# A planned attention and ReGLU kernel: blocks of 2 and 4 tiles, transposing transfers one tile earlier, and a planner with other due times

## The chip, the cores and the metric

The kernel runs on one core of one Trainium2 chip. The metric is the device time of one execution in microseconds (us), less is better. The kernel before takes 240.97 us, the median of three runs (240.74 to 241.13).

## The reference, cut to what matters

Chunked attention with memory rows on 4 batches of 8 heads, 768 positions of 64 values; then a gated feed-forward layer on the 3072 rows of 512 that come out.

```
for c in range(nc):                       # 24 chunks of 32 positions
    q_c = q[:, :, c_start:c_end]
    k_full = concat([mem_k, k[:, :, c_start-16 : c_end+8]])     # 8 + up to 56 keys
    v_full = concat([mem_v, v[:, :, c_start-16 : c_end+8]])
    a = softmax(q_c @ k_full.T / 8)
    out[:, :, c_start:c_end] = a @ v_full
x = out as 3072 rows of 512
return (relu(x @ w_gate) * (x @ w_val)) @ w_out    # 512 -> 1536 -> 512
```

## The kernel before

The 3072 rows are 24 tiles of 128, six to a batch of the reference. A tile `a` passes through these steps, and the names are those of the planner's list:

- `qk`: two loads on POOL's queue, k and q of the tile, cast to bf16 on the way (`load_qk`, L257). Batch 0 (tiles 0 to 5) has its own loads of pairs.
- `t`, `tc`: k and q turned so that the head's 64 values lie on partitions. Up to tile 10 TensorE does it (`qk_t`, L279, four transposes each for k and for q), and ACT or DVE copies the result out of PSUM. From tile `LATE_QK` = 11 on one transposing transfer on SP's queue does both (`qk_transfer`, L283), and only the copy of the keys into `kT` is left, `tc`, on ACT or DVE (L79, L81).
- `s`: scores, 32 small matmuls (L310). They need the copied keys of the tile and of the one behind it, because a chunk sees 8 keys to its right.
- `max`, `sub`, `exp`, `sum`, `rec`, `nrm`: softmax on DVE and ACT.
- `p`, `pc`: P turned. Up to tile 9 on TensorE with a copy (L359), from `LATE_P` = 10 on by a transposing transfer on SP (`p_transfer`, L363).
- `v`, `x`: values, 16 matmuls (L389; batch 0 has its own form), copied to `xT`.

Values stand in two large tiles `v_bd`, one for each parity of the batch. For a batch POOL issues two large loads and two small ones (`vl`, `ve`, L184), and eight copies of the memory's rows (`mr`, L167; batch 1's on SP). From the loads, 16 copies on ACT or DVE (`up`, `upper`) fill the rows that chunks share. The loads of batch 3 come only when tile 11's values are through; a small memset on DVE (`hold`, L684) that the planner puts behind tile 17's `tc` keeps them back further.

The feed-forward layer goes by blocks of 2 or 4 tiles. For a block, 24 products `f` (gate and value in turn, L408; four matmuls of 256 or 512 columns each) go through four PSUM slots (`fps`); a relu on ACT frees the gate's slot (L414), a multiplication on DVE the value's (L420). Then the products `o` with the second weights, in triples of matmuls (L433), four triples to a tile, through the same slots; ACT copies each tile out and stores it (`oc`, L79, L440). The slots go round in the order of use: a product takes the slot of the one four before it.

The order of everything is written by a planner in the kernel, when it is built. It goes through modelled time with a cost for each step, and gives each free engine the step of highest priority whose operands are due by its estimates. What comes out is one fixed order for each engine. On the chip each engine takes its instructions in this order and waits where an operand isn't there; the modelled times play no part any more. For a load the estimate is the end of a modelled queue plus a constant; for a transposing transfer the end of the same queue, and its users are due `LAND` or `LAND_P` us after that:

```
LAND = {a: 4.0 if a < 16 else 3.5 if a < 19 else 2.0 for a in range(NT)}
LAND_P = {a: 3.0 if a < 14 else 2.5 if a < 18 else 2.0 for a in range(NT)}
...
queue_end = max(queue_end, t + 1.5) + {"t": 2.6, "pc": 1.3}[key[0]]
done[key] = queue_end + 1.0
```

SP holds, after a few loads and the eight rows of batch 1, only transposing transfers. `pace` keeps the transposes on PE of later tiles from coming too early, by the place of their block; `pace_t` keeps a transfer behind the scores of five tiles before.

Of the kernel before, what the change touches and what calls it, by code (L numbers as in the profile page):

```python
# [19 lines left out]
def kernel(  # L20
# [27 lines left out]
    KW = CH + NMEM  # L48
    CTX = 16 + CH + 8
    NSET = 2  # L50
    BLOCKS = [2, 2, 2, 4, 4, 4, 4, 2]
    GROUPS = [(0, 2), (2, 6), (6, 9), (9, 12)]
    BAND0 = 48
    UT = 3

    LATE_QK, LATE_P = 11, 10

    KEY_RUNS = ((0, CH, 0), (KW, 64, CH), (CH, KW, CTX))
    assert sum(BLOCKS) == NT and NMEM == 8 and D == 64 and H == 8
# [455 lines left out]


    ISSUE, SLACK = 1.5, 1.0
    LAND = {a: 4.0 if a < 16 else 3.5 if a < 19 else 2.0 for a in range(NT)}
    LAND_P = {a: 3.0 if a < 14 else 2.5 if a < 18 else 2.0 for a in range(NT)}

    def pace_t(a):
        return [("s", a - 5)]
# [136 lines left out]
    load_v_nat(5)  # L659
    for par in range(2):  # L660
        load(("vm", par), 256, 0.3, lambda par=par: mem_values(par))
    for a, i in late[:5]:
        load_qk_op(a, i)
    for i in range(2):
        load(("wo", i), 768, 4.1, lambda i=i: load_out(i))
    for b in range(1, B):
        deps = ([("z0", hp, c0) for hp in range(HP) for c0 in range(0, NCH, 8)] if b > 1 else [("z1", hp) for hp in range(HP)]) + ([("v", TPB * (b - NSET + 1) - 1)] + ['hold'] if b > NSET else [])
        if b == 1:
            for n in range(2 * HP):
                op(("mr", b, n), {"SP": 0.72}, lambda e, b=b, n=n: mem_rows(nc.sync, b, n),  # L670
                   deps + [(("vm", 0), 0.2), (("vm", 1), 0.2)], (0,))
        for par in range(2):
            load_v_op(b, par, deps)
        if b == 2:
            for n in range(2 * HP):
                load(("mr", 2, n), 192, 0.22, lambda n=n: mem_rows(nc.gpsimd, 2, n),
                     deps + [(("vm", 0), 0.2), (("vm", 1), 0.2)])
        for a, i in late[(5, 20, 26)[b - 1]:(20, 26, 36)[b - 1]]:
            load_qk_op(a, i)
    for n in range(2 * HP):  # L680
        load(("mr", 3, n), 192, 0.22, lambda n=n: mem_rows(nc.gpsimd, 3, n),
             deps + [(("vm", 0), 0.2), (("vm", 1), 0.2)])

    op("hold", {"DVE": 0.1}, lambda e: nc.vector.memset(v_bd[1][0:2 * CH, 0, 0, :].bitcast(F32), 0.0), [("v", 2 * TPB - 1)],  # L684
       prio=(0,), after=[("tc",17,1)])
# [6 lines left out]
    def schedule():  # L692
        done, started, times = {}, set(), [0.7]
        free = {e: 0.7 for e in ("PE", "ACT", "DVE", "SP", "POOL")}
        queue_end, flying, gives = 0.0, [], [(WARM + 0.15, "fps")]
        room["fps"] -= 1
        heapq.heappush(times, WARM + 0.15)
        todo = {e: [] for e in free}
        order, n_load = [], 0
        names = lambda o: [d[0] if timed(d) else d for d in o["deps"]] + o["after"]  # L700
        missing = {k: len(set(names(o))) for k, o in ops.items()}
        users = {}
        for k, o in ops.items():
            for d in set(names(o)):
                users.setdefault(d, []).append(k)

        def offer(k):
            for e in ops[k]["eng"]:
                bisect.insort(todo[e], (ops[k]["prio"], k), key=lambda x: x[0])

        for k in ops:
            if not missing[k]:
                offer(k)

        def ready(o, t, margin=0.0):
            if any(d not in started for d in o["after"]):
                return False
            for d in o["deps"]:
                d, lag = d if timed(d) else (d, 0.0)
                if d not in done or done[d] + lag + margin > t + 1e-9:  # L720
                    return False
            return all(room[r] >= o["take"].count(r) for r in o["take"])

        while len(started) < len(ops) + len(loads):
            t = heapq.heappop(times)
            while times and times[0] <= t + 1e-9:
                heapq.heappop(times)
            for g in [g for g in gives if g[0] <= t + 1e-9]:
                gives.remove(g)
                room[g[1]] += 1  # L730
            flying = [f for f in flying if f > t]
            moved = True
            while moved:
                moved = False
                for e in ("POOL", "PE", "ACT", "DVE", "SP"):
                    if free[e] > t + 1e-9:
                        continue
                    if e == "POOL":
                        if n_load == len(loads):
                            continue  # L740
                        o = loads[n_load]
                        if len(flying) >= 8 or not ready(o, t):
                            continue
                        n_load += 1
                        key = o["key"]
                        if o["n"]:
                            end = t + 0.62 + 0.27e-3 * o["n"]
                            queue_end = max(queue_end, end + 0.8) + o["work"]
                            flying.append(queue_end + 1.0)
                            done[key] = queue_end + (1.2 if n_load < 8 else 4.5 if key[:2] == ("vl", 1) else 2.4 if n_load < 45 else 6.0 if key[0] == "vl" else 4.0)  # L750
                        else:
                            end = done[key] = t + max(o["work"], 0.6)
                        fn = o["fn"]
                    else:
                        o = None
                        soon = False
                        for _, key in todo[e]:
                            late_pe = e == "PE" and t > 36.0 and ops[key]["prio"][0] == 1
                            if ready(ops[key], t, MARGIN if late_pe else 0.0):
                                o = None if soon and key[0] in ("up", "z0") else ops[key]  # L760
                                break
                            soon = soon or ready(ops[key], t + 0.3)
                        if o is None:
                            if e == "PE" and 1.3 < t < WARM:
                                order.append((t, lambda: idle_product(256)))
                                free[e] = t + (0.213 if t < 9.0 else 0.11)
                                heapq.heappush(times, free[e])
                            elif e == "PE" and t <= 1.3:
                                heapq.heappush(times, 1.31)
                            continue  # L770
                        for x in o["eng"]:
                            todo[x].remove((o["prio"], key))
                        d = o["eng"][e]
                        d, lat = d if isinstance(d, tuple) else (d, d)
                        d *= (1.8 if e == "PE" and t < 8.0 and key[0] in ("t", "p", "sh", "f") else 1.0)
                        end = t + d
                        done[key] = end + 0.25 if e == "PE" else t + lat + 0.08

                        if e == "SP" and key[0] in ("t", "pc"):
                            queue_end = max(queue_end, t + 1.5) + {"t": 2.6, "pc": 1.3}[key[0]]  # L780
                            done[key] = queue_end + 1.0
                        elif queue_end > t and key[0] == "oc":
                            queue_end += 0.7
                        fn = lambda o=o, e=e: o["fn"](e)
                        for g in o["give"]:
                            g, lag = g if isinstance(g, tuple) else (g, 0.0)
                            gives.append((done[key] + lag, g))
                            heapq.heappush(times, done[key] + lag)
                    for r in o["take"]:
                        room[r] -= 1  # L790
                    started.add(key)
                    for k in users.get(key, ()):
                        missing[k] -= 1
                        if not missing[k]:
                            offer(k)
                    order.append((t, fn))
                    free[e] = end
                    lags = {d[1] for k in users.get(key, ()) for d in ops[k]["deps"] if timed(d) and d[0] == key}
                    for x in [end] + [done[key] + lag + m for lag in lags | {0.0, 0.2, 1.5} for m in (0.0, MARGIN)]:
                        heapq.heappush(times, x)  # L800
                    moved = True
            assert times, [k for k in ops if k not in started][:20]
        return order
# [33 lines left out]
```

## Time and profile before

| | |
|---|---|
| median of three runs | 240.97 us |
| the profiled execution | 240.65 us |
| its span on the core | 238.9 us |
| granted TensorE clock | 0.998 |
| PE, DVE, ACT, POOL busy | 232.5, 145.3, 135.5, 77.4 us |
| transposing transfers on SP | 13 of q and k, 14 of P |
| first product of tiles 6 to 9, 10 to 13, 14 to 17, 18 to 21 (us from the span's start) | 85.47, 120.61, 153.93, 188.99 |

PE is TensorE's matmuls, ACT ScalarE, DVE VectorE, POOL GpSimd and SP SyncE; L with a number is a line of the kernel before. The duration of a matmul includes its way through the array, so durations of neighbours overlap, and it is the distance from one start to the next that adds up to the span. An idle time in square brackets names what ended the wait before an instruction.

### The profile page before, as it was taken

Reading aid. Unit: us, or ns where it says so; the run is one execution under the profiler, and the core shown is the slowest. Engines: PE = TensorE matmul, PEld = TensorE weight load, DVE = VectorE, ACT = ScalarE, POOL = GpSimd, SP = SyncE. Lnnn points to the kernel's source line nnn. Section 1 sums busy time; section 2 is a strip of 40 time slices with the busy share of each in tenths; the row PEclk is TensorE's granted clock in tenths of the full one; section 3 lists DMA queues with packets and bytes.
Section 4 is the critical chain, followed back from the end, with each engine's and each line's share of the span. In section 5 each row is a group of like instructions: output and inputs, shape, how many; then the busy total and the mean of one; then the engine's idle time right before and its main releaser. Section 6 shows DMA issues by size and latency. Waiting matters only on the chain.

```text
span 238.9 us, 6437 instructions
## 1 busy us (share of the span) xinstructions
PE 232.5 (97%) x2654; PEld 137.7 (58%) x2654; DVE 145.3 (61%) x292; ACT 135.5 (57%) x284; POOL 77.4 (32%) x102
## 2 busy tenths in 40 slices
PE   7898999999999999999999999999999999999994
PEld 5577887785589644455544444444555444445873
DVE  6674876987888389994279851599960043410430
ACT  7577777866885456897566851365523233312422
POOL 8975779313920374700094552100000000000000
PEclk9999999999999999999999999999999999999999
DMA  6999999999999999996199999995121300012102
GB/s 74 171 179 202 201 166 161 206 133 125 190 166 138 131 156 118 122 129 136 70 141 101 135 154 91 113 209 64 27 43 47 127 4 0 0 47 88 44 3 88
DMA packets 103069, 26.88 MB, mean 113 GB/s; under 512 B 94080, under 2 KB 99968, under 8 KB 103040
## 3 DMA queue, kind: packets, MB, share of 16 engines
q0 software_dynamic: 76128, 14.65, 92.7%
q1 hardware_dynamic: 23312, 5.53, 23.2%
q10 hardware_dynamic: 3600, 6.29, 8.4%
q8 instruction: 21, 0.34, 0.7%
q14 instruction: 8, 0.07, 0.2%
HBM read 28.55 MB, written 6.29 MB: 146 GB/s over the span
## 4 chain that ended last, share of the span: by engine, by line
PE 93%; DMA 2%; POOL 2%; issue 1%; ACT 1%; ACTq 0%; POOLq 0%
PE v_ps L408 27%; PE g_ps L408 26%; PE out_ps L433 26%; PE xT_ps L389 3%; PE s_ps L310 2%; DMA v_n<-in_v_dram 2%; PE idle_ps L140 2%; PE vs_ps L216 2%; PE xT_ps L382 2%; PE qk_ps L279 1%; PE pT_ps L359 1%; POOL qk_p L229 1%; PE qk_ps L238 1%; PE xT_ps L375 1%; POOL v_n L200 0%
## 5 line engine op out<-in xcount | busy, mean ns | idle before, releaser
L420 DVE TENSOR_TENSOR gvT<-v_ps,g_relu 128x256 f16<-128x256 f32 (+1 forms) x96 | 53.0, 554 | 48.7 <-PE v_ps L408 35.1
L408 PE MATMUL v_ps<-xT,w_val_sb 128*128 128x256 f16 (+1 forms) x384 | 78.2, 326 | 0.1
L408 PE MATMUL g_ps<-xT,w_gate_sb 128*128 128x256 f16 (+1 forms) x384 | 78.1, 326 | 0.0
L414 ACT ACTIVATE g_relu<-g_ps 128x256 f16<-128x256 f32 (+1 forms) x96 | 47.0, 490 | 41.5 <-PE g_ps L408 39.8
L433 PE MATMUL out_ps<-w_out_sb,gvT 128*128 128x512 f16 (+2 forms) x300 | 65.8, 371 | 0.0
L408 PEld LDWEIGHTS <-w_gate_sb 128*128 128x128 f16 x384 | 36.9, 98 | 24.8
L408 PEld LDWEIGHTS <-w_val_sb 128*128 128x128 f16 x384 | 35.9, 98 | 22.5 <-issue 0.5
L433 PEld LDWEIGHTS <-gvT 128*128 128x128 f16 x300 | 27.6, 97 | 29.5
L79 ACT COPY o_sb<-out_ps 128x512 f32<-128x512 f32 (+2 forms) x25 | 14.2, 568 | 29.6 <-PE out_ps L433 19.4
L323 DVE TENSOR_REDUCE mx<-s_ps 128x8 f32<-128x512 f32 x24 | 16.4, 685 | 13.9 <-PE s_ps L310 13.5
L338 ACT ACTIVATE p_exp<-dif 128x256 f16<-128x256 f32 (+2 forms) x72 | 19.6, 339 | 6.3 <-DVE dif L330 6.1
L184 POOL DMA_DIRECT2D v_bd<-in_v_dram x12 | 11.0, 924 | 33.6 <-DVE v_bd L684 19.2
L342 DVE TENSOR_REDUCE sm<-p_exp 128x8 f32<-128x512 f16 x24 | 16.4, 683 | 5.0 <-ACT p_exp L338 4.8
L257 POOL DMA_DIRECT2D qk_b<-in_k_dram x18 | 16.2, 902 | 9.7 <-DMA v_bd<-in_v_dram 5.4
L257 POOL DMA_DIRECT2D qk_b<-in_q_dram x18 | 16.2, 899 | 9.7 <-DMA v_bd<-in_v_dram 7.2
L79 ACT COPY v_bd<-v_bd 24x768 f16<-24x768 f16 (+1 forms) x23 | 18.5, 823 | 1.2 <-ACT o_sb L79 0.9
L353 DVE TENSOR_TENSOR p_n<-p_exp,rinv 128x512 f16<-128x512 f16 x24 | 16.5, 686 | 0.3
L330 DVE TENSOR_TENSOR dif<-s_ps,mx 128x512 f32<-128x512 f32 x24 | 16.2, 674 | 0.2
L79 ACT CAST xT<-xT_ps 128x512 f16<-128x512 f32 x17 | 10.0, 586 | 8.5 <-PE xT_ps L389 7.3
L167 POOL DMA_DIRECT2D v_bd<-vmem x16 | 10.2, 645 | 12.4 <-DMA qk_b<-in_q_dram 6.1
L140 PE MATMUL idle_ps<-idle 128*128 128x256 bf16 x69 | 11.3, 314 | 1.1 <-DVE warm L477 1.1
L389 PEld LDWEIGHTS <-v_bd 128*128 128x128 f16 x288 | 9.8, 96 | 3.6
(60 smaller groups left out, 165.6 us busy)
## 6 DMA issues: line engine op xcount, KB each, us to landing
out_dram<-o_sb ACTq DMA_DIRECT2D x23, 256.0 KB
qk_b<-in_k_dram POOLq DMA_DIRECT2D x18, 128.0 KB, 8.0
qk_b<-in_q_dram POOLq DMA_DIRECT2D x18, 128.0 KB, 8.9
v_bd<-in_v_dram POOLq DMA_DIRECT2D x6, 384.0 KB, 11.2
w_out_sb<-in_moe_w_out_dram POOLq DMA_DIRECT2D x2, 768.0 KB, 10.5
qk_p<-in_k_dram POOLq DMA_DIRECT2D x3, 256.0 KB, 5.3
qk_p<-in_q_dram POOLq DMA_DIRECT2D x3, 256.0 KB, 6.3
v_n<-in_v_dram POOLq DMA_DIRECT2D x6, 128.0 KB, 6.5
```

What stands on the lines that cost most here:

```text
L79: nc.scalar.copy(o, i)
L257: nc.gpsimd.dma_start(qk_b[a][:, 1 - i], bass.AP(tensor=x.tensor, offset=x[b, 0, 128 * t, 0].offset, ap=[[D, 128], [S * D, H], [1, D]]))
L323: nc.vector.reduce_max(SM[a, "mx"], s4, axis=AX.X)
L330: nc.vector.tensor_tensor(out=SM[a, "dif"].rearrange("p (m r) a s -> p r m a s", r=2), in0=S_ps.pop(a).rearrange("p r (m a) s -> p r m a s ...
L338: nc.scalar.activation(p[:, :, :, s0:s0 + k1 - k0], dif[:, :, :, k0:k1], ACT.Exp, scale=SCALE)
L342: nc.vector.reduce_sum(SM[a, "sm"], SM[a, "p"], axis=AX.X)
L353: nc.vector.tensor_tensor(out=P_n[a], in0=SM.pop((a, "p")), in1=rinv_b, op=ALU.mult)
L389: nc.tensor.matmul(ps[:, hp, r], lhsT=v_bd[b % NSET][:, hp, 4 * t + g, :], rhs=x[:, hp, r], start=True, stop=True)
L408: nc.tensor.matmul(ps, lhsT=w[:, f, 128 * m:128 * m + 128], rhs=xTs[blk][:, f, :], start=(f == 0), stop=(f == NFC - 1))
L414: nc.scalar.activation(st["r", m], st.pop((0, m)), ACT.Relu)
L420: nc.vector.tensor_tensor(out=st["gv"][:, m, :], in0=st.pop((1, m)), in1=st.pop(("r", m)), op=ALU.mult)
L433: nc.tensor.matmul(st["o", t, c], lhsT=st["gv"][:, m, 128 * t:128 * t + 128], rhs=w_out_sb[:, m, c[0]:c[1]], start=(m == 0), stop=(m == ND ...
```

## The change

The list of blocks splits tiles 6 to 9 into 2 + 2. Transposing transfers do q and k from tile 10 and P from tile 9, so there are 14 and 15 of them. The order of loads becomes a list (`ORDER`: numbers are loads of k or q, `w` a half of the second weights, `v` the values of a batch, `m` its memory rows): batch 2's values now stand after 18 loads of k and q where they stood after 20, batch 3's after 26 in both. The planner's estimates change: a new rule with `turn` for when a transposing transfer ends, users due 4.5 us (`t`) and 3.5 us (`pc`) after it, and smaller constants behind loads. `pace` is as it was, but its lead of 44 us for blocks from the fifth on now holds for tiles 8 and 9.

```diff
-    BLOCKS = [2, 2, 2, 4, 4, 4, 4, 2]
+    BLOCKS = [2,2,2,2,2,4,4,4,2]
...
+    ORDER = [5, 'w0', 'w1', 'v1', 13, 'v2', 'm2', 8, 'v3', 10, 'm3']
...
-    LATE_QK, LATE_P = 11, 10
+    LATE_QK, LATE_P = 10, 9
...
-    LAND = {a: 4.0 if a < 16 else 3.5 if a < 19 else 2.0 for a in range(NT)}
-    LAND_P = {a: 3.0 if a < 14 else 2.5 if a < 18 else 2.0 for a in range(NT)}
+    LAND = {a: 4.5 for a in range(NT)}
+    LAND_P = {a: 3.5 for a in range(NT)}
...
+    def v_deps(b):
+        z = [("z0", hp, c0) for hp in range(HP) for c0 in range(0, NCH, 8)] if b > 1 else [("z1", hp) for hp in range(HP)]
+        return z + ([("v", TPB * (b - NSET + 1) - 1), "hold"] if b > NSET else [])
+    def mem_deps(b):
+        return v_deps(b) + [(("vm", 0), 0.2), (("vm", 1), 0.2)]
...
+    for step in ORDER:
+        if isinstance(step, int):
+            for a, i in late[n_qk:n_qk + step]:
+                load_qk_op(a, i)
+            n_qk += step
+            continue
...
-                            done[key] = queue_end + (1.2 if n_load < 8 else 4.5 if key[:2] == ("vl", 1) else 2.4 if n_load < 45 else 6.0 if key[0] == "vl" else 4.0)
+                            done[key] = queue_end + (1.2 if n_load < 8 else 4.5 if key[:2] == ("vl", 1) else 2.4 if n_load < 45 else 3.5 if key[0] == "vl" else 2.5)
...
-                            queue_end = max(queue_end, t + 1.5) + {"t": 2.6, "pc": 1.3}[key[0]]
-                            done[key] = queue_end + 1.0
+                            double = key[0] == "t"
+                            busy = queue_end > t + 1.2
+                            begin = max(t + 1.2 + (3.0 if busy else 0.2), turn)
+                            if queue_end > begin:
+                                turn = begin + (3.8 if double else 2.7)
+                                queue_end += 1.6 if double else 0.9
+                            else:
+                                turn = begin + (1.5 if double else 0.9)
+                            done[key] = turn + 0.3
```

The fixed order that the planner writes is the same as before on PE up to the second block's out products (60 us in the profile). Some places where it differs after that, with tiles in brackets:

| engine | before | after |
|---|---|---|
| ACT, first steps of tiles 14 to 17's block | exp(18), oc(13), relu 0, exp(19), relu 1, tc(22), relu 2, exp(20), relu 3, tc(23) | exp(18), tc(22), oc(13), relu 0, exp(19), relu 1, tc(23), exp(20), relu 2 |
| DVE | max(15), sub(15), hold | max(14), sub(14), hold |
| copies `up` of batch 3's second load, in the block of tiles 10 to 13 | from relu 7 on ACT and gate 6 on DVE on | from relu 4 and gate 4 on |
| SP | t(11 to 15), pc(10 to 13), t(16), pc(14), t(17, 18), pc(15 to 17), t(19 to 23), pc(18 to 23) | t(10 to 14), pc(9 to 12), t(15), pc(13), t(16 to 18), pc(14 to 17), t(19 to 23), pc(18 to 23) |
| PE, scores and values around 114 to 122 us | s(14) far ahead, v(14), s(15), s(16), block of 10 to 13 | v(13), s(14), s(15), s(16), block of 10 to 13, in it v(14) |

More of the change, by code (lines that the diff above doesn't have):

```diff
@@ L661 @@
         load(("vm", par), 256, 0.3, lambda par=par: mem_values(par))
[L662 to L668, printed above, removed]
-            for n in range(2 * HP):
[L670 to L682, printed above, removed]
+    def v_deps(b):
[3 more added lines that the diff above has]
+        return v_deps(b) + [(("vm", 0), 0.2), (("vm", 1), 0.2)]
+    n_qk = 0
+    for step in ORDER:
[4 more added lines that the diff above has]
+            continue
+        kind, b = step[0], int(step[1])
+        if kind == "w":
+            load(("wo", b), 768, 4.1, lambda b=b: load_out(b))
+        elif kind == "v":
+            for par in range(2):
+                load_v_op(b, par, v_deps(b))
+        else:
+            for n in range(2 * HP):
+                load(("mr", b, n), 192, 0.22, lambda b=b, n=n: mem_rows(nc.gpsimd, b, n), mem_deps(b))
+    if "m1" not in ORDER:
+        for n in range(2 * HP):
+            op(("mr", 1, n), {"SP": 0.72}, lambda e, n=n: mem_rows(nc.sync, 1, n), mem_deps(1), (0,))
     op("hold", {"DVE": 0.1}, lambda e: nc.vector.memset(v_bd[1][0:2 * CH, 0, 0, :].bitcast(F32), 0.0), [("v", 2 * TPB - 1)],
@@ L694, in schedule @@
         free = {e: 0.7 for e in ("PE", "ACT", "DVE", "SP", "POOL")}
-        queue_end, flying, gives = 0.0, [], [(WARM + 0.15, "fps")]
+        queue_end, turn, flying, gives = 0.0, 0.0, [], [(WARM + 0.15, "fps")]
         room["fps"] -= 1
@@ L779, in schedule @@
                         if e == "SP" and key[0] in ("t", "pc"):
-                            queue_end = max(queue_end, t + 1.5) + {"t": 2.6, "pc": 1.3}[key[0]]
-                            done[key] = queue_end + 1.0
+                            double = key[0] == "t"
[4 more added lines that the diff above has]
+                                queue_end += 1.6 if double else 0.9
+                            else:
+                                turn = begin + (1.5 if double else 0.9)
+                            done[key] = turn + 0.3
                         elif queue_end > t and key[0] == "oc":
```

## The prediction

> **What bounds the kernel now.** First the busy shares and the chain of work that ended last, from the page:
>
> ```profile
> PE 232.5 (97%) x2654; PEld 137.7 (58%) x2654; DVE 145.3 (61%) x292; ACT 135.5 (57%) x284; POOL 77.4 (32%) x102
> ...
> PE 93%; DMA 2%; POOL 2%; issue 1%; ACT 1%; ACTq 0%; POOLq 0%
> ```
>
> TensorE is the bound. Busy shares hide small gaps, so I then read the distance from start to start in the timeline of PE (start, duration, line, shapes, count):
>
> ```profile
> 46.55 0.60 PE L408 MATMUL g_ps<-xT,w_gate_sb 128*128 128x256 f16 x4
> ...
> 49.61 0.39 PE L375 MATMUL xT_ps<-pT,vmem 128*128 128x128 f16 x4
> ...
> 50.53 0.40 PE L359 MATMUL pT_ps<-band,p_n 128*128 128x128 f16 x4
> 50.77 0.60 PE L408 MATMUL v_ps<-xT,w_val_sb 128*128 128x256 f16 x4
> ...
> 56.05 0.61 PE L279 MATMUL qk_ps<-ident_b,qk_b 128*128 128x128 bf16 x8
> 56.50 3.40 PE L433 MATMUL out_ps<-w_out_sb,gvT 128*128 128x512 f16 x15
> ```
>
> From 46.55 to 49.61 stand seven products of a block of 2 tiles: 3.06 / 7 = 0.437 us each (a product is four matmuls). Four transposes of P take 50.77 - 50.53 = 0.24 us, eight of q and k 56.50 - 56.05 = 0.45. The chain of waits (start, length, work) gives a block of 4:
>
> ```profile
> 188.99 0.86 PE g_ps L408 x4
> ...
> 209.71 10.36 PE out_ps L433 x48
> ```
>
> 24 products in 20.72 us, 0.863 each. I laid such distances against every step from 60 us to the end: all small excesses together are 0.3 us. So the time is the sum of PE's work; no stall is left to remove, but any operand that comes late adds to it in full.
>
> Which operands come close? In the view of who waited for whom (total us, times, longest) and the timelines of ACT, DVE and POOL:
>
> ```profile
> ACT kT L79 <- DMA qk_T<-qk_b: 2.3, 2, 1.5
> DVE v_bd L81 <- DMA v_bd<-in_v_dram: 1.0, 1, 1.0
> ```
>
> ```profile
> 154.13 0.59 ACT L79 COPY o_sb<-out_ps 128x512 f32<-128x512 f32 x1 [0.41 <-PE out_ps L433]
> ...
> 158.61 0.62 ACT L79 COPY kT<-qk_T 128x512 bf16<-128x512 bf16 x1 [0.77 <-DMA qk_T<-qk_b]
> 159.13 0.59 ACT L414 ACTIVATE g_relu<-g_ps 128x512 f16<-128x512 f32 x1
> ...
> 162.75 0.62 ACT L79 COPY kT<-qk_T 128x512 bf16<-128x512 bf16 x1 [1.49 <-DMA qk_T<-qk_b]
> ```
>
> ```profile
> 118.00 0.69 DVE L330 TENSOR_TENSOR dif<-s_ps,mx 128x512 f32<-128x512 f32 x1
> 118.64 0.11 DVE L684 MEMSET v_bd<- 64x64 f32 x1
> ```
>
> ```profile
> 119.43 3.65 POOL L184 DMA_DIRECT2D v_bd<-in_v_dram x4 [19.22 <-DVE v_bd L684]
> ...
> 133.80 0.87 POOL L257 DMA_DIRECT2D qk_b<-in_k_dram x1 [5.14 <-DMA v_bd<-in_v_dram]
> ```
>
> The copies of kT for tiles 22 and 23 already wait on ACT for their transposing transfers, which land at 158.6 and 162.7. They stand behind two and four relus of the next block, with nothing urgent behind them. The last batch's values are held by the memset at 118.64, issued at 119.43, and the second of the two large loads has landed at 133.8.
>
> **The change part by part.** (1) Tile 10's q and k and tile 9's P leave PE: -0.45 - 0.24 = -0.69 us of the path. (2) Tiles 6 to 9 as 2 + 2: 48 products of 0.437 for 24 of 0.863, 20.98 - 20.72 = +0.26; out products are the same 300. The extra 12 relus on ACT and 12 gates on DVE lie beside PE's work; what shrinks is cover: four PSUM slots are 4 x 0.437 = 1.75 us of products instead of 3.45, if an engine is held up there. Sum of PE: -0.43. The bounds of the split are +0.07 (the shortest distance in the trace, 0.433) and +0.26, so PE lies between -0.62 and -0.43; I take the larger cost, which is the usual distance. (3) Two more transfers on SP. SP's queue has nothing else to delay but its own later transfers, below. (4) The loads' order, the pace (which now takes 44 us of lead for tiles 8 and 9 too) and the planner's estimates cost no instruction; they decide where each user stands behind its transfer or load. Transfers are estimated by a new rule with 4.5 and 3.5 us behind it, but loads with 3.5 and 2.5 for 6.0 and 4.0. So I followed each through the new order; up to 60 us PE's order is the old one.
>
> Tiles 9 to 13: in the trace the first four transposing transfers are issued from 65.1 to 74.2 us and are all there by some 81 us; the new first one is issued some 2.5 us earlier, when its loads are there, and its users stand at 76 us and after. Cover enough: nothing.
>
> Batch 3's values: the hold now stands behind the difference of tile 14, in place of tile 15. In the trace it comes 118.64 - 116.78 = 1.86 us after the scores it follows. The new scores of tile 14 stand 7 triples of out products (0.647 each), three scores (0.24) and two changes of shape (0.1) ahead of the next block, whose start moves from 120.61 to 119.8 (-0.43, and the values of tile 14 with 0.40, which move behind it): 119.8 - 5.5 = 114.3. The hold is then at 116.2: 2.4 us earlier than 118.64, and with it the loads behind it on POOL. But P of tile 14, landed before these loads in the trace, now is sent with them. How much it delays the queue the trace doesn't show for this place; bounds: 0, if its packets fill gaps, and 2.0 us, for 512 packets at the rate from 144 to 162 us (4591 in 18 us). They go out early in a stretch of 40 us whose first 6 us the trace's transposes spent without a packet (below), so I take a quarter, 0.5.
>
> Tile 22's kT copy: landing 158.6 - 2.4 + 0.5 = 156.7 (156.2 to 158.2). On ACT it now stands *ahead of* the last output copy of tiles 10 to 13 and of the next block's first relu, and right behind the exponents of tile 18, which are done near 153 (152.90 + 0.82 in the trace, less the gain); before, it stood behind both and one more relu. So ACT waits over 3 us, and the output copy behind it keeps its PSUM slot: free at 156.7 + 0.52 + 0.59 + 0.05 = 157.9. The product that needs this slot is the fourth of its block, by PE's sum at 153.93 - 0.43 + 3 x 0.863 + 0.24 + 0.1 = 156.4. Stall: 1.5 us (1.0 to 3.0); none if tile 22 landed by 155.2. Tile 23 lands 4.1 us behind, 160.8; the relu behind its copy and an exponent is done at 162.7, its slot wanted at 162.6: 0.1.
>
> Batch 3's shifted copies (`upper`): those of the second load stand now behind the fifth relu of the block and one copy (119.8 + 4 x 1.73 + 0.34 + 0.86 for its product, 0.8 for relu and its start, 0.83: 129.6) on ACT and close to it on DVE; the landing is 133.8 - 2.4 = 131.4 (to 133). The relu behind is done at 131.4 + 0.83 + 0.6 = 132.8, the slot wanted at 119.8 + 7 x 1.73 + 0.34 = 132.2. Stall 0.6 (0 to 2). It makes PE later but not the transfers, so it is taken off tile 22's stall, not added.
>
> Sum: -0.43 + 1.5 + 0.1 = +1.2 us (-0.6 with nothing late, +2.7 at the upper ends) on the profiled run's 240.65 (span 238.9 and 1.75 around it): 241.8. The runs' median lies 0.32 above it: 242.1.
>
> **Where a rule would decide otherwise.** Transposing transfers beside loads are held up here:
>
> ```profile
> q0 software_dynamic: 3486, 0.44, 115.1%
> q10 hardware_dynamic: 168, 0.28, 14.0%
> ...
> pT<-p_n SPq DMA_TRANSPOSE x1
> ```
>
> This is the DMA view from 120 to 126 us: one transpose was issued (at 122.35), and the loads' queue moved 3486 packets, the transposes' queue q1 none. The Trainium skill, "DMA: Bandwidth & Descriptors", Queues, rings and completion order, says that each DMA engine goes round the queues that have work, packet by packet. By that, P of tile 14 would get its share at once and tiles 19 to 23 would come sooner; the time would be that of the first rival. The row shows a transfer waiting some 4 us for its first packet, so I go by the row.
>
> **The rivals.** *Nothing is late*: the transfers' queue is emptier when tiles 19 to 22 are sent, and tile 22 lands by 155.2. For it: every user in the middle of the new order has several us. Against: its landing would have to move 3.4 us where its loads move 2.4. Time 240.97 - 0.43 = 240.5 (240.3 to 240.7): chance 0.20, half of it under the bound of faster. *The wait about cancels the gain*: ACT's wait is there, but tile 22 lands at 155.4 to 156.1, a stall of 0.2 to 0.9: 240.7 to 241.4, chance 0.17 (0.04 of it below 240.5, should the split cost less). *PE itself waits for P*: values 14 and 15 stand at 132 and 135 us in PE's order. P of tile 15 was sent at 122.35 and landed at 131; with tile 14's P ahead of it in the same loads it would be 133 to 136, and PE, which takes nothing past a waiting instruction, is held 0 to 1.5 us beyond tile 22's stall: 242.6 to 244, chance 0.11. It decides once P takes more than 12 us from issue to landing. The forecast, 241.5 to 243.0: 0.52.
>
> **How the numbers follow.** Under 0.2% (0.48 us, 240.49 to 241.45) a measurement can't be told from no change. Faster: 0.10 + 0.04 = 0.14. Same: the rest of the first rival, 0.10, and of the second, 0.13: 0.23. Slower: 0.52 + 0.11 = 0.63. Range: 240.4, which takes in the stall-free case and leaves out its lower end, to 243.3; some 0.15 lies outside. The likeliest case alone has 241.5 to 243.0.
>
> **What would show it.** ACT's timeline: one kT copy ahead of an output copy at 154 to 157 us with 2 to 4 us of idle time put down to qk_T. PE: a gap of over 0.7 us in the first products of tiles 14 to 17, and the start of tiles 10 to 13 at 119.8. The last loads of v_bd issued near 117.0. Transposes on PE: qk_ps from qk_b x32 for 40, pT_ps x36 for 40. Wrong, if ACT doesn't wait there, or if PE's last out product comes at 235.0 or sooner.

## The result and the profile after

The changed kernel takes 244.0 us, the median of four runs (243.79 to 244.08); the kernel before takes 241.05 beside it (240.74 to 241.8). The ratio is 1.0116 [1.0092, 1.0141]: slower by 2.95 us. The profiled execution took 244.08 us, its span is 242.3 (before: 240.65 and 238.9). The page has the busy shares and the shares of the chain that ended last:

```profile
PE 233.6 (96%) x2738; PEld 146.5 (60%) x2738; DVE 146.3 (60%) x299; ACT 139.9 (58%) x299; POOL 77.9 (32%) x102
...
PE 83%; ACT 6%; DVE 2%; DMA 2%; issue 2%; POOL 2%; ACTq 1%; DVEq 0%; POOLq 0%
```

ACT had 1% of the chain before and has 6% now, and DVE 2%. So there are stretches in which PE is not the bound. The groups of instructions show that PE does lose the work that the change takes from it (before, both groups had x40):

```profile
L360 PE MATMUL pT_ps<-band,p_n 128*128 128x128 f16 x36 | 3.5, 220 | 0.0
L280 PE MATMUL qk_ps<-ident_b,qk_b 128*128 128x128 bf16 x32 | 2.8, 220 | 0.0
```

To find the stretches I took the new order of PE, gave each step the start-to-start distance that it has in the trace of before, and looked where the real start falls further behind. PE's last out product starts at 238.19 us for 235.43, 2.76 later. That is -0.44 of PE's own work, +0.24 in the first 45 us, where the two orders are the same, and +2.96 of stalls. The other 0.67 of the 3.43 us between the two profiled executions come behind PE's work: from that start to the span's end there are 4.12 us for 3.45, and 3.8 to 3.9 in the profiles of the other kernels below, so this part goes with the execution and not with the change. The stalls, by their place:

| at (us) | what PE was about to do | excess (us) |
|---|---|---|
| 68.8, 69.6 | first products of tiles 4 and 5 | 0.20 + 0.36 |
| 94.7 | a gate product of tiles 6 and 7 | 0.11 |
| 105.3, 106.6, 107.8, 109.05 | gate products of tiles 8 and 9 | 0.36 + 0.36 + 0.36 + 0.31 |
| 161.7, 166.5 | scores of tiles 21 and 22 | 0.18 + 0.66 |

(0.06 is spread over the rest.) The largest group is in tiles 8 and 9, a block that the change makes. PE's timeline (start, duration, line, shapes, count, idle time and what ended it):

```profile
104.52 0.60 PE L409 MATMUL v_ps<-xT,w_val_sb 128*128 128x256 f16 x4
105.32 0.60 PE L409 MATMUL g_ps<-xT,w_gate_sb 128*128 128x256 f16 x4 [0.20 <-ACT g_relu L415]
105.78 0.60 PE L409 MATMUL v_ps<-xT,w_val_sb 128*128 128x256 f16 x4
106.58 0.60 PE L409 MATMUL g_ps<-xT,w_gate_sb 128*128 128x256 f16 x4 [0.20 <-ACT g_relu L415]
107.04 0.60 PE L409 MATMUL v_ps<-xT,w_val_sb 128*128 128x256 f16 x4
107.84 0.60 PE L409 MATMUL g_ps<-xT,w_gate_sb 128*128 128x256 f16 x4 [0.20 <-ACT g_relu L415]
```

From gate product to gate product there are 1.26 us, where two products should take 0.874. The brackets show only 0.20 of each 0.39, since for the rest the row of the product before still runs (104.52 + 0.60). ACT's timeline has the other side:

```profile
103.88 0.59 ACT L80 COPY o_sb<-out_ps 128x512 f32<-128x512 f32 x1
104.50 0.34 ACTq L441 DMA_DIRECT2D out_dram<-o_sb  x1
104.88 0.38 ACT L415 ACTIVATE g_relu<-g_ps 128x256 f16<-128x256 f32 x1 [0.41 <-PE g_ps L409]
105.29 0.83 ACT L80 COPY v_bd<-v_bd 24x768 f16<-24x768 f16 x1
106.14 0.38 ACT L415 ACTIVATE g_relu<-g_ps 128x256 f16<-128x256 f32 x1
106.55 0.83 ACT L80 COPY v_bd<-v_bd 24x768 f16<-24x768 f16 x1
```

ACT alternates relu and shifted copy, with no idle time. A pair takes it 106.14 - 104.88 = 1.26 us, the very rhythm of PE. So ACT sets the pace there: PE makes a gate and a value product in 0.87 us, but ACT gives a gate's slot back every 1.26. Before, copies of the same batch stood among the relus of the block of 4:

```profile
100.65 0.60 ACT L414 ACTIVATE g_relu<-g_ps 128x512 f16<-128x512 f32 x1
101.27 0.83 ACT L79 COPY v_bd<-v_bd 24x768 f16<-24x768 f16 x1
102.12 0.60 ACT L414 ACTIVATE g_relu<-g_ps 128x512 f16<-128x512 f32 x1
```

There a pair takes ACT 1.47 us, less than the 1.73 that PE takes for two products of a block of 4. In the new block ACT starts late too, because an output copy and the issue of its store stand ahead of the first relu. From 103.88 to 104.88 they take 1.0 us: 0.59 of copy, then 0.34 of issue, which shows as idle time in the next row. At 69 us that does it, right behind an exponent:

```profile
68.14 0.56 ACT L80 COPY o_sb<-out_ps 128x512 f32<-128x512 f32 x1
68.73 0.34 ACTq L441 DMA_DIRECT2D out_dram<-o_sb  x1
69.11 0.38 ACT L415 ACTIVATE g_relu<-g_ps 128x256 f16<-128x256 f32 x1 [0.42 <-PE g_ps L409]
```

The gate product for this relu had started at 67.02. The relu ended at 69.49, and the product that takes over its slot started at 69.55, 0.36 late. Before, PE had other work at this place, eight transposes (0.54 us) between the first two products of tiles 4 and 5:

```profile
66.68 0.60 PE L408 MATMUL g_ps<-xT,w_gate_sb 128*128 128x256 f16 x4
67.12 0.71 PE L279 MATMUL qk_ps<-ident_b,qk_b 128*128 128x128 bf16 x8
67.66 0.60 PE L408 MATMUL v_ps<-xT,w_val_sb 128*128 128x256 f16 x4
```

They are the last transposes of q and k in PE's order, those of tile 10, which the change gives to SP. So what it takes off PE was also cover for ACT.

The third place is the forecast one. ACT's timeline at the first steps of tiles 14 to 17, which answers to the kT copies shown of before:

```profile
154.16 0.82 ACT L339 ACTIVATE p_exp<-dif 128x256 f16<-128x256 f32 x3 [0.41 <-DVE kT L82]
156.67 0.62 ACT L80 COPY kT<-qk_T 128x512 bf16<-128x512 bf16 x1 [1.70 <-DMA qk_T<-qk_b]
157.20 0.58 ACT L80 COPY o_sb<-out_ps 128x512 f32<-128x512 f32 x1
...
158.20 0.60 ACT L415 ACTIVATE g_relu<-g_ps 128x512 f16<-128x512 f32 x1 [0.43 <-PE s_ps L311]
```

Tile 22's copy waits 1.70 us for its transfer and starts at 156.67; the output copy and the first relu stand behind it. The next step is on DVE, whose first gate needs that relu:

```profile
158.83 0.69 DVE L421 TENSOR_TENSOR gvT<-v_ps,g_relu 128x512 f16<-128x512 f32 x1 [1.22 <-ACT g_relu L415]
...
160.85 0.69 DVE L331 TENSOR_TENSOR dif<-s_ps,mx 128x512 f32<-128x512 f32 x1
```

Behind this gate stand the softmax steps of a tile, down to the difference at 160.85 that gives back the PSUM slot of the scores. PE wants that slot for the next scores:

```profile
161.69 0.32 PE L311 MATMUL s_ps<-kT,qk_T 64*32 64x64 bf16 x32
...
166.54 0.32 PE L311 MATMUL s_ps<-kT,qk_T 64*32 64x64 bf16 x32 [0.59 <-DVE dif L331]
```

So the wait on ACT reaches PE by way of DVE, and through the slot of the scores, not through a slot of the products.

### The profile page after: what moved, and what is told of

Read it like the earlier page. It is cut to its first block, busy times and chain, and to the rows that moved or that the text cites. A ratio compares the mean times of both kernels' runs of the same rounds, so it can differ in the third digit from the quotient of the medians.

```text
span 242.3 us, 6650 instructions
## 1 busy us (share of the span) xinstructions
PE 233.6 (96%) x2738; PEld 146.5 (60%) x2738; DVE 146.3 (60%) x299; ACT 139.9 (58%) x299; POOL 77.9 (32%) x102
## 4 chain that ended last, share of the span: by engine, by line
PE 83%; ACT 6%; DVE 2%; DMA 2%; issue 2%; POOL 2%; ACTq 1%; DVEq 0%; POOLq 0%
PE v_ps L409 24%; PE out_ps L434 24%; PE g_ps L409 24%; PE xT_ps L390 2%; DMA v_n<-in_v_dram 2%; PE s_ps L311 2%; PE idle_ps L141 2%; ACT v_bd L80 2%; PE vs_ps L217 2%; PE xT_ps L383 2%; ACT o_sb L80 1%; ACT g_relu L415 1%; POOL qk_p L230 1%; PE qk_ps L239 1%; PE pT_ps L360 1%
## 5 line engine op out<-in xcount | busy, mean ns | idle before, releaser
L421 DVE TENSOR_TENSOR gvT<-v_ps,g_relu 128x256 f16<-128x256 f32 (+1 forms) x108 | 54.7, 510 | 57.9 <-PE v_ps L409 38.9
L409 PE MATMUL g_ps<-xT,w_gate_sb 128*128 128x256 f16 (+1 forms) x432 | 80.2, 308 | 1.0 <-ACT g_relu L415 1.0
L409 PE MATMUL v_ps<-xT,w_val_sb 128*128 128x256 f16 (+1 forms) x432 | 80.2, 308 | 0.2
L415 ACT ACTIVATE g_relu<-g_ps 128x256 f16<-128x256 f32 (+1 forms) x108 | 48.8, 455 | 45.3 <-PE g_ps L409 43.9
L409 PEld LDWEIGHTS <-w_gate_sb 128*128 128x128 f16 x432 | 41.0, 98 | 21.4 <-issue 1.8
L409 PEld LDWEIGHTS <-w_val_sb 128*128 128x128 f16 x432 | 41.2, 98 | 20.1 <-issue 0.7
L80 ACT COPY v_bd<-v_bd 24x768 f16<-24x768 f16 (+1 forms) x25 | 20.3, 821 | 1.6 <-ACT o_sb L80 0.9
L258 POOL DMA_DIRECT2D qk_b<-in_k_dram x18 | 16.7, 926 | 10.2 <-PE xT_ps L383 5.1
```

Of the source, the lines that this page charges most:

```text
L80: nc.scalar.copy(o, i)
L258: nc.gpsimd.dma_start(qk_b[a][:, 1 - i], bass.AP(tensor=x.tensor, offset=x[b, 0, 128 * t, 0].offset, ap=[[D, 128], [S * D, H], [1, D]]))
L409: nc.tensor.matmul(ps, lhsT=w[:, f, 128 * m:128 * m + 128], rhs=xTs[blk][:, f, :], start=(f == 0), stop=(f == NFC - 1))
L415: nc.scalar.activation(st["r", m], st.pop((0, m)), ACT.Relu)
L421: nc.vector.tensor_tensor(out=st["gv"][:, m, :], in0=st.pop((1, m)), in1=st.pop(("r", m)), op=ALU.mult)
```

## The experiments

The theories were these. The split itself is the cost: in blocks of 2 tiles, ACT's relus and what stands between them are slower than PE. Or the planner's new estimates are: the smaller constants behind loads let the shifted copies of a batch stand among the relus, and the new ends of transfers put kT copies ahead of relus. Later runs ask what ACT's steps really cost against the planner's price, and whether P comes late. Each time is a median with its lowest and highest run; the ratio is to the kernel before, which had medians of 240.99 to 241.02 beside them. It comes from all runs and isn't the quotient of the medians.

**The blocks alone**, in the kernel before:

```diff
-    BLOCKS = [2, 2, 2, 4, 4, 4, 4, 2]
+    BLOCKS = [2,2,2,2,2,4,4,4,2]
```

> The kernel before with the new list of blocks alone (transfers, loads and estimates as before). PE's sum: +0.26 us. Theory A (ACT is too full in blocks of 2 tiles: a relu of 0.41 us per pair of products that PE makes in 0.87, with a shifted copy of 0.83 between two relus the pair takes ACT 1.25, and PE has only four small slots ahead): three such pairs stand in the order here, so a loss of 0.5 to 1.5 us, 241.5 to 242.5, with PE gaps of 0.36 before gate products of tiles 8 and 9. Theory B (copies stand too close behind their loads) and theory C (transposing transfers come late): +0.1 to +0.4 us, 241.1 to 241.5, no such gaps.

242.52 us (242.43 to 242.63), 1.0057 [1.0038, 1.0076]. That is 1.53 us, half as much as the change loses, without any of its other parts. The largest excesses are 0.55 at 68.1 us, where PE waits for a copy of qT that ACT does late, and 0.34 at 107.0, a gate product of tiles 8 and 9. ACT alternates relu and copy here too (108.12 to 109.38, 1.26 us), but PE doesn't fall into this rhythm: a stretch of values in its order, at 107.45, gives ACT time.

**The old constants behind loads**, in the changed kernel:

```diff
-  ... 2.4 if n_load < 45 else 3.5 if key[0] == "vl" else 2.5)
+  ... 2.4 if n_load < 45 else 6.0 if key[0] == "vl" else 4.0)
```

> The changed kernel with the planner's old, longer constants behind loads (6.0 and 4.0 us). Theory B: ACT and DVE no longer wait for batch 2's and 3's values and nothing piles up; most of the 3 us comes back, 240.8 to 242. Theory A: only the pairs of relu and copy count; two stand in tiles 8 and 9 in place of three, so 0.4 to 0.8 us come back, 243.2 to 243.6. Theory C: within 0.3 of 244.0.

242.56 us (242.43 to 242.98), 1.0062 [1.0041, 1.0082]: 1.44 less than the change. The stalls in tiles 8 and 9 are 0.81 for 1.39, those at 161 to 166 us are gone, the one at 69 stays (0.51), and a new one of 0.62 stands ahead of the scores of tile 16. So the constants are a part of it, and neither theory has the whole.

**The old estimate of transposing transfers** (`LAND`, `LAND_P` and the rule for `queue_end` as before), in the changed kernel:

```diff
-    LAND = {a: 4.5 for a in range(NT)}
-    LAND_P = {a: 3.5 for a in range(NT)}
+    LAND = {a: 4.0 if a < 16 else 3.5 if a < 19 else 2.0 for a in range(NT)}
+    LAND_P = {a: 3.0 if a < 14 else 2.5 if a < 18 else 2.0 for a in range(NT)}
...
+                            queue_end = max(queue_end, t + 1.5) + {"t": 2.6, "pc": 1.3}[key[0]]
+                            done[key] = queue_end + 1.0
```

> The changed kernel with the old estimate of a transfer's end and the old LAND and LAND_P. Tile 22's copy stands behind three relus again. Theory C (the wait for tiles 22 and 23 costs the time): 241 to 242. Theory A: three pairs of relu and copy are still there in tiles 8 and 9, so the 1.4 us at 105 to 109 stay: 243 to 244. Theory B: within 0.5 of 244.0.

243.66 us (243.55 to 243.97), 1.0106 [1.0086, 1.0126], 0.34 less. The stalls at 161 to 166 us are gone, but there is one of 1.11 at 122.3, where the first product of tiles 10 to 13 waits for the values of tile 13. The stalls in the blocks of 2 are much as in the change (0.54 at 69, 1.02 at 106 to 109). So the old rule costs in one place about what the new one costs in another, and the rule is not what makes the difference.

**The later half of batch 2's shifted copies on DVE only**, in the changed kernel:

```diff
-  {"ACT": 0.16 + 64 * 0.9e-3 * (i1 - i0), "DVE": 0.1 + 64 * 0.55e-3 * (i1 - i0)},
+  {"DVE": 0.1 + 64 * 0.55e-3 * (i1 - i0)} if b == 2 and m == 1 else {...},
```

> The changed kernel, but the second half of batch 2's shifted copies may go on DVE alone (0.35 us each there), so that no copy stands between the relus of tiles 8 and 9 on ACT. Theory A: the four gaps of 0.36 us at 105 to 109 go, 1.0 to 1.5 us faster than the changed kernel: 242.5 to 243.0. Theories B and C: within 0.4 of 244.0, since the waits for loads and transfers are untouched.

242.8 us over six runs (241.7 to 244.03), 1.006 [1.0034, 1.0087]. The stalls at 105 to 109 us are gone: it was these copies that filled ACT. But the profiled execution took 244.03, as long as the change. Its ACT timeline, and then its PE timeline:

```profile
156.81 0.62 ACT L80 COPY kT<-qk_T 128x512 bf16<-128x512 bf16 x1 [2.90 <-DMA qk_T<-qk_b]
```

```profile
161.87 0.32 PE L311 MATMUL s_ps<-kT,qk_T 64*32 64x64 bf16 x32 [0.95 <-DVE dif L331]
...
166.72 0.32 PE L311 MATMUL s_ps<-kT,qk_T 64*32 64x64 bf16 x32 [0.58 <-DVE dif L331]
```

Tile 22 lands where it did (156.81 for 156.67), but the wait for it is 2.90 us for 1.70, and the stalls at the scores of tiles 20, 21 and 22 are 0.36, 1.02 and 0.65 for 0.84 together. PE came there earlier and waited for the same landing. In this execution 1.19 of the 1.39 us cured at 105 are paid here, and a wait of 0.35 at 60.7, for the load of a q, takes more than the rest. The other five runs are 0.7 to 2.3 us shorter; the median gains 1.2, and the change alone had runs within 0.3 us of each other. So the payment seems to vary from run to run, and only the profiled one shows its place.

**More room behind the transfers of tiles 20 on**, in the changed kernel:

```diff
-    LAND = {a: 4.5 for a in range(NT)}
+    LAND = {a: 4.5 if a < 20 else 7.0 for a in range(NT)}
```

> The changed kernel, but the users of the transfers of tiles 20 to 23 are due 7.0 us behind the estimated end, not 4.5; up to 140 us every order is the same. Tile 22's copy then stands behind the next block's first relu. Theory C (this wait holds the relu, the gate and so the next scores): the gaps before the scores of tiles 21 and 22 (0.2 and 0.7 us) go, 0.6 to 1.0 us faster than the changed kernel: 243.0 to 243.4. Theory A (ACT too full in tiles 8 and 9): the gaps at 105 to 109 are untouched, and if they alone make the time, 243.9 to 244.1.

242.76 us (242.51 to 242.92), 1.0072 [1.0057, 1.0087], 1.24 less than the change. Tile 22's copy now stands behind the first relu and waits for nothing. The stalls at 161 to 166 us are gone, those at 105 to 109 all there (1.45), and the one at 69 too (0.37).

**ACT's steps at higher prices** in the planner, in the changed kernel. An output copy and its store go from 0.58 to 0.98 us (the trace has 1.0), a shifted copy from 0.85 to 0.99. The trace has 0.85 for a shifted copy alone (105.29 to 106.14), but 1.26 for the pair of relu and copy, where the planner counted 0.28 + 0.85:

```diff
-                op(("oc", blk, t, c), {"ACT": (d[0] + 0.1, d[1])},
+                op(("oc", blk, t, c), {"ACT": (d[0] + 0.5, d[1])},
...
-                op(("up", b, n, m), {"ACT": 0.16 + 64 * 0.9e-3 * (i1 - i0), ...
+                op(("up", b, n, m), {"ACT": 0.30 + 64 * 0.9e-3 * (i1 - i0), ...
```

> The changed kernel with two costs of the planner raised to what the trace shows on ACT: an output copy with its store 1.0 us for 0.58, a shifted copy 1.0 for 0.86. Theory D (the planner counts ACT's work too low, so ACT runs behind its plan where outputs and copies follow each other, and blocks of 2 tiles have too little cover for it): the gaps at 69 and at 105 to 109 us shrink by half or more, 0.8 to 1.6 us faster than the changed kernel: 242.4 to 243.2, unless tiles 21 and 22 take it back (theory C: the earlier PE is, the longer it waits there). Theory A without D (blocks of 2 with a copy between two relus lose whatever the plan says): three such pairs remain in tiles 8 and 9, gaps of 0.36 there, 243.5 to 244.

241.87 us over ten runs (240.69 to 243.03), 1.0033 [1.0012, 1.0053]: 2.1 of the 2.95 us come back with two prices, which weren't tried apart. In the profiled execution the stall at 69 is gone, one of 0.30 is left at 105.6, and one of 0.32 ahead of the scores of tile 21. The runs differ by more than 2 us. The profiled one (241.22) is one of the short ones, so it doesn't show what the long ones wait for; the seventh and the ninth experiment bear on that.

**Copies on DVE and more room together** (the edits of the fourth and fifth experiments):

> Both cures together: the second half of batch 2's shifted copies on DVE alone, and 7.0 us behind the transfers of tiles 20 to 23. If A and C are the two places that cover each other: no gaps at 105 to 109 nor before the scores of 20 to 22, 1.9 to 2.6 us faster than the changed kernel, 241.4 to 242.1, and the runs no longer spread from 241.7 to 244.0. If something else holds PE back as soon as it is earlier (values of P on their transfers, theory E): 242.5 to 243.5 with PE gaps before values.

241.39 us over ten runs (nine of them 241.06 to 241.45, one 242.68), 1.0019 [1.0003, 1.0034]. Together they gain 2.6 us (1.2 each alone): only 0.38 at 69 us and 0.11 at 94.5 are left. And the runs are close again but for one, where the fourth experiment's, without the room, were spread over 2.3 us: so it was most likely the wait for these transfers that varied there.

**The earlier transfers alone**, in the kernel before with its old blocks:

```diff
-    LATE_QK, LATE_P = 11, 10
+    LATE_QK, LATE_P = 10, 9
```

> The kernel before with the transfers one tile earlier alone (tile 10's q and k, tile 9's P), blocks as before. If the split of tiles 6 to 9 is what makes room for the transfer: the block of tiles 6 to 9 starts only when tile 9's P is there, among batch 2's loads, and PE stands idle for 5 to 15 us before it: 246 to 256. If the parts are independent: -0.7 us, 240.3.

256.75 us, two runs, 1.0654 [1.0631, 1.0676]. Who PE waited for (total, times, longest):

```profile
PE s_ps L310 <- DVE rinv L346: 7.2, 3, 2.6
PE s_ps L310 <- DVE dif L330: 4.8, 2, 4.4
```

PE waits 2.2 to 4.4 us before the scores of tiles 11, 12, 13 and 14. The old block of tiles 6 to 9 needs the values of tile 9 for its first product, and tile 9's P now comes by a transfer, issued at 89.60, whose last packets move between 95 and 97 us. The planner has put the scores of four tiles ahead of those values, and scores have one PSUM slot, so PE goes through them at the pace of softmax on DVE. The first product of the block starts at 100.95 where it started at 85.47. Another 1.7 us are lost behind the wait: the first two products take 1.66 and 1.71 us from start to start where such a product took 0.863, and the granted clock is 0.50 from 100.95 to 104.3, where it was 1.00 from 78 to 85. With 2 + 2 the products of tiles 6 and 7 run meanwhile (from 85.19 in the changed kernel). So the two parts of the change are coupled: the transfers one tile earlier need the split.

**ACT's costs and more room together** (the edits of the fifth and sixth experiments):

> The changed kernel with the raised costs of ACT's output and shifted copies and with 7.0 us behind the transfers of tiles 20 to 23. If theories C and D name the two places and they only cover each other: no gap at 69, at most 0.3 at 105, none before the scores of 20 to 22, PE's last out product near 235.2; 240.6 to 241.0, and the spread of the run with the costs alone (240.7 to 243.0) is gone. If something else holds PE as soon as both are away: 241.3 to 242.5.

241.05 us over twelve runs (240.72 to 241.34) against 241.02 of 29 runs: 0.9996 [0.9983, 1.001]. All of the loss is gone, and the spread of the sixth experiment (2.3 us) with it (0.6), by the same room. One stall of 0.30 at 105.7 is left, where the relus of tiles 8 and 9 still alternate with shifted copies twice. PE's last out product starts at 235.31 (before 235.43): most of the 0.43 us that PE saves goes to this stall and to a first stretch that is 0.2 later in this execution (45.75 for 45.55), and 0.12 is left, less than can be measured. The list of loads, the pace, the new rule for transfers and the smaller constants behind loads are all in this kernel, so none of them costs under these prices and this room; under the old ones only the rule and the constants were tried.

**The same with batch 2's copies on DVE**:

> As the run before it, and the second half of batch 2's shifted copies on DVE alone. C and D: the last gap at 105 goes too, PE's sum of -0.43 us comes out whole, 240.4 to 240.8. If DVE, which has 0.35 us more for each of five copies, now holds a gate: 240.8 to 241.3, with a gap put down to a gate at 100 to 112 us.

241.33 us (240.76 to 242.24), 1.0012 [0.9997, 1.0027]. The stall at 105.7 is gone, and a new one of 0.62 stands ahead of the scores of tile 16 at 120.3: no gain.

**ACT's costs, and still more room** (`LAND` 8.0 from tile 19 on, `LAND_P` 4.5):

> The changed kernel with the raised costs, and all transfers' users later: 8.0 us for tiles 19 to 23, 4.5 for every P. More room behind P: if late P were still costing (theory E), 0.3 to 0.6 us faster than the run with 7.0 us; if not, the values only come later, the same within 0.3, 240.6 to 241.2.

241.0 us over twelve runs (240.48 to 243.44), 1.0011 [0.9985, 1.0037]. More room behind P gives nothing that can be measured, so a late P is not what holds the kernel. Two runs are over 2 us longer than the median; the profiled execution is one of them, at a granted clock of 0.993 (the ninth experiment's profile has 1.000), so I read no mechanism from it.

No version beats the kernel before by more than can be measured.

## Why the prediction was right in direction and wrong in size

The direction was right; the 1.2 us of the sum are 2.95, and the time lies above the range.

**PE's own work: right.** -0.43 was forecast and -0.44 is there, by the distances of before. The split costs PE's array what was said.

**The failed step: "The extra 12 relus on ACT and 12 gates on DVE lie beside PE's work", at nothing.** The same sentence names what was at stake, four slots worth "1.75 us instead of 3.45, if an engine is held up there", and then I didn't follow ACT's order through tiles 4 to 9 as I did from tile 14 on. What it put at nothing measured 0.56 + 0.11 + 1.39 = 2.06 us of stalls. For tiles 8 and 9 the sum could have been made from rows of before: the working had 0.83 us for a shifted copy, and with a relu of 256 columns behind it (0.38) that is more than the 0.874 us of two products. Each such pair takes 0.39 us of the cover (1.26 - 0.87), and the output copy ahead of the first had used it up. A quarter of it (0.56) is in tiles 4 and 5, a block of 2 before too. There the orders are new: an exponent stands right ahead of the output copy on ACT, and tile 10's transposes no longer give it 0.54 us. The working counted these transposes as gain alone. The planner counts an output copy with its store at 0.58 us where ACT is held 1.0, and a relu with a shifted copy at 1.13 where they take 1.26; with both prices raised most of the loss is gone (241.87). So the split isn't bad of itself: it is a block with less cover, under an order whose prices for ACT are too low.

**"Cover enough: nothing" for tiles 9 to 13: right.** PE waits for no transposing transfer or its copy there, though the first one was issued only 0.65 us earlier (64.41 for 65.06) and not 2.5.

**Batch 3's loads and tile 22's landing: the number came true by another way, which is luck.** The forecast was the last loads near 117.0 us and the landing 1.9 before that of the old kernel, at 156.7. The landing came at 156.67. But tiles 10 to 13 started at 122.17 us, not at 119.8, because of the stalls ahead of them. With that the hold came at 118.57 and not at 116.2, and POOL's timeline shows the loads no earlier than before (119.43):

```profile
119.74 3.67 POOL L185 DMA_DIRECT2D v_bd<-in_v_dram x4 [16.06 <-ACT p_exp L339]
...
132.08 0.91 POOL L258 DMA_DIRECT2D qk_b<-in_k_dram x1 [3.38 <-DMA v_bd<-in_v_dram]
```

The second large load had landed by 132.08 for 133.80: from its own issue it took 10.2 us where it took 12.3, and why it was quicker I didn't separate. Transposing transfers are held up beside loads as the forecast had it. The DMA view from 122 to 124 us of the changed kernel, where a P transfer was issued at 122.23, has

```profile
q0 software_dynamic: 2021, 0.26, 201.8%
```

and no row for q1; its first 167 packets come between 124 and 126 us, the first 2.7 us behind the issue. For the P transfer issued at 162.77, with nothing on the loads' queue, it is 1.2 us. The Trainium skill, "DMA: Bandwidth & Descriptors", Queues, rings and completion order, has the engines go round the queues that have work, packet by packet; this row doesn't show that. Tile 22 landed at 156.67, not by 155.2 as the rival with that rule would have it.

**Tile 22's copy ahead of the output copy and the relu: right in mechanism, off in size and victim.** ACT waited 1.70 us, not over 3, and PE lost 0.84, not 1.5. Tiles 14 to 17 started at 155.89, 2.4 us later than the forecast's 153.5 (153.93 - 0.43), which took away part of the wait; with the stalls at 105 us gone and the same landing, ACT waited 2.90 and PE lost 2.0 (the fourth experiment's profile). I had the slot of the fourth product as the victim; it was that of the scores, by way of DVE's first gate. So the lateness from the failed step made this one smaller: its price depends on when PE comes, and a sum of separate terms has no place for that.

**Tile 23 and batch 3's shifted copies: no stall of PE** (0.1 and 0.6, the latter not added). DVE waited once 1.5 us for these loads, and PE didn't feel it.

**The rivals.** Nothing late: false. A wait that about cancels the gain: tile 22's stall (0.84) is of the size that it gave, but the time isn't, since the 2.06 us of tiles 4 to 9 stand beside it. PE waiting for P: not seen; the values of tiles 14 and 15 start at 134.61 and 137.60 us without a gap, and more room for P gained nothing. The mechanism that decided, ACT's rhythm in blocks of 2, was not among them.

## What to carry to other kernels

For a bound engine that hands its results to another through a few buffers, don't compare busy shares: write down the second engine's order for one turn of the buffers, with all that stands between, and compare its period with the first one's. A transfer that an engine issues for its own result belongs to the price of that result, here 1.0 us and not 0.58. Where a stall waits for a moment that doesn't move with the bound engine, curing an earlier stall can feed it, so try the cures together before judging either.

## What of the hardware was not expected

An output copy of 128 x 512 on ACT takes 0.59 us, but with the store that ACT issues behind it 1.0 us pass until the next instruction starts (103.88 to 104.88); the issue takes 0.34. The second large load of batch 3's values was issued at 121.25 in the one kernel and at 121.56 in the other, and landed 12.3 and 10.2 us later: two us of difference in the same load, whose cause no run here separates. And after 15 us in which PE was busy for 2.4 (85.6 to 100.9 in the eighth experiment), its next eight matmuls ran at a granted clock of 0.50, at about half their usual pace.
